# New priority offsets for the static planner of a gated linear attention and a four-expert layer

## The chip, the cores and the metric

The kernel runs on one core of one Trainium2 chip. The metric is the device time of one execution in microseconds (us); the time given is the median of three runs. The engines are named as the profile names them: PE (TensorE, with PEld for its weight loads), DVE (VectorE), ACT (ScalarE), POOL (GpSimd) and SP (SyncE, which here only issues transfers).

## The reference

Two layers stand one behind the other. The first is a gated linear attention with a 48 x 48 state for each of 4 batches and 8 heads over 768 steps; the second mixes four experts with weights that are known from the start.

```python
f = 1.0 / (1.0 + np.exp(-f_logit))
for t in range(S):                                   # S = 768
    state = f[:, :, t, :, None] * state + np.einsum('bhd,bhe->bhde', k[:, :, t], v[:, :, t])
    y[:, :, t] = np.einsum('bhd,bhde->bhe', q[:, :, t], state)
...
x = np.ascontiguousarray(y.transpose(0, 2, 1, 3)).reshape(B * S, H * D)      # 3072 x 384
p = domain_probs / (domain_probs.sum(-1, keepdims=True) + 1e-09)
for e in range(E):                                   # E = 4
    h = np.maximum(x @ w1[e], 0.0)                   # 384 -> 1024
    out += p[:, e:e + 1] * (h @ w2[e])               # 1024 -> 384
```

## The kernel before

**Tiling.** The 768 steps are cut into six chunks c = 0 to 5 of 128 steps. A chunk holds four batches b = 0 to 3, and each batch gives one tile of 128 tokens of 384 columns.

**Steps of the attention**, named `step c.b`:

- `gate1`, `gate2` (L311, L315, ACT) make the logarithm of the gate. `cs` (L319, PE) sums it over the steps into one PSUM bank. `exps` (L339, ACT, two activations for each batch, a third one, L341, in chunk 0) reads that bank and frees it.
- `q` and `k` (L347, POOL or DVE) multiply by these exponentials. `tp` turns both with a transposing transfer (L360, SP queue); in chunk 0 and half of chunk 1, `tpq`, `tpk` (L356, PE) and `ev_tp` do that.
- `at` (L383, PE) makes the scores of one batch or of a pair of batches, two PSUM banks for each batch. `ev_at0` and `ev_at1` (L387, DVE) put the mask on and free the banks.
- `y` (L394 and L398, PE) needs both `ev_at` steps of its batch. `ev_ys` (L370 on ACT, L372 on DVE) scales y by the expert weights; `xs` (L375, SP queue) turns the result into the experts' input with a transposing transfer.
- `kv` (L404, PE), `ev_kv` (L411, two instructions on DVE) and four `sf` (L416, L419, POOL) move the state on; `egs` is a small transfer for the state's factor.

**Steps of the experts.** In chunk 0 and half of chunk 1 these are `h` (L432, PE), `relu` (L443 on ACT, L441 on DVE), `o` (L447, PE), `ev_o` (L454). From the second half of chunk 1 on the work goes in groups of half a chunk and a pair of experts: `hs` (L464, PE, six matmuls of 256 columns), `relu_s` (L472 on ACT, L470 on DVE), four sums `s1` to `s4` (L482, DVE), seven products `p` (L501, PE, eight matmuls of 192 columns each), `ev_p` (L509 on DVE, L272 on ACT), and `store` (L513, SP queue). `hs c.hf.p...` reads the `xs` of both batches of half `hf`.

**What sets the order.** The function adds some 1,470 steps to a planner. A step has a cost for each engine that may run it, a priority, the steps that it depends on, and the buffers that it takes and frees. `Plan.run` goes through time: whenever an engine is free, it takes the ready step of the lowest priority. The finished list is then recorded once, so every engine gets a fixed sequence of instructions and runs it in that order on the chip, with semaphores between the engines. The planner's times decide the order and, where a step may run on several engines, the engine; on the chip nothing is chosen. PSUM is one ring of eight banks, `ps_m`; each step on PE that makes a result takes banks, and the reader of the result gives them back.

Two things tune the planner by hand. `MOVES` is a list of offsets to priorities: `cs 5.3=10.3` makes that step later, and `k 0.2=46.8@DVE` also nails the engine. And a dependency between two engines counts `LATENCY` (0.2) and the `lag` of its producer; the steps of chunk 0 on ACT and DVE carry 0.1 more:

```python
for o in self.ops:
    if o.name.split(" ")[-1].startswith("0.") and set(o.costs) & {"ACT", "DVE"}:
        o.lag += 0.1
```

**Fill-in matmuls.** Until the first `h` the recorded program puts matmuls on a constant tile (L873, 512 columns) into PE's planned pauses; their number comes from the planner's times.

## Time and profile before

| | |
|---|---|
| median of three runs | 288.67 us (288.63 to 288.93) |
| the profiled execution | 288.44 us, its span 286.7 us |
| PE busy | 280.0 us (98% of the span), 3,010 matmul records |
| DVE, ACT, POOL busy | 195.5, 180.7, 112.0 us |
| transfers | 41.85 MB |
| granted TensorE clock | 1.0 |

The profile is one execution; its span runs from the first to the last instruction, and its own time is 1.7 us longer than the span. Each digit of a row of slices is the busy share of a fortieth of the span in tenths. A group's line gives engine, line of the kernel, shapes, count, then busy time and the mean time of one instruction in ns, then the idle time of the engine before them. In the timeline, instructions of one kind that follow each other on an engine are merged into one row (start, length, count). A matmul's record runs on into its successors' by the depth of the pipeline, so what a matmul costs TensorE is read from start to start: 0.109 us for 256 columns, 0.082 us for 192.

### The profile page before, as it was taken

How to read it: one execution, taken by the hardware profiler on the slowest of the kernel's cores; microseconds unless marked ns; L12 is line 12 of the kernel's file. 1: busy time of each engine (PE TensorE's matmuls, PEld its weight loads, DVE VectorE, ACT ScalarE, POOL GpSimd, SP SyncE). 2: the span in 40 equal slices, each digit the busy share in tenths (PEclk: the TensorE clock that was granted, in tenths of full speed). 3: DMA queues.
4: the chain of work that ended last, by engine and by line, in shares of the span. 5: the costliest groups of instructions: out<-in, count | busy, mean ns of one | idle time of the engine just before them, and what ended most of it. 6: DMA issues, size and time to landing. Idle time of an engine off the chain costs nothing.

```text
span 286.7 us, 7475 instructions
## 1 busy us (share of the span) xinstructions
PE 280.0 (98%) x3010; PEld 235.7 (82%) x3016; DVE 195.5 (68%) x385; ACT 180.7 (63%) x343; POOL 112.0 (39%) x181
## 2 busy tenths in 40 slices
PE   7999999999999999999999999999999999999994
PEld 2567555567786999998999999999999999998994
DVE  4595122778698868846889876888885787630683
ACT  5847683758776846867695657375865544659500
POOL 5796500218763762478157258134373000000000
PEclk9999999999999999999999999999999999999999
DMA  7999999997998989999889999995254143420011
GB/s 154 206 173 206 207 195 201 181 198 167 176 184 161 213 154 211 128 222 195 177 182 171 126 219 179 222 184 112 58 132 90 28 84 83 88 56 2 2 55 55
DMA packets 157782, 41.85 MB, mean 146 GB/s; under 512 B 148124, under 2 KB 156956, under 8 KB 157748
## 3 DMA queue, kind: packets, MB, share of 16 engines
q1 hardware_dynamic: 146500, 34.66, 63.7%
q0 software_dynamic: 11248, 6.72, 16.5%
q8 instruction: 23, 0.38, 0.6%
q14 instruction: 11, 0.09, 0.1%
HBM read 31.51 MB, written 4.72 MB: 126 GB/s over the span
## 4 chain that ended last, share of the span: by engine, by line
PE 93%; SPq 2%; DMA 2%; DVE 1%; issue 0%; ACT 0%; DVEq 0%
PE ps_m L464 33%; PE ps_m L501 29%; PE ps_m L447 11%; PE ps_m L432 11%; SPq L282 2%; PE ps_m L383 2%; PE ps_m L398 2%; DMA q<-in_q_dram 2%; PE ps_m L394 1%; PE ps_m L404 1%; PE ps_m L319 1%; PE ps_m L356 1%; DVE AT L387 0%; ACT QK L272 0%; PE ps_m L423 0%
## 5 line engine op out<-in xcount | busy, mean ns | idle before, releaser
L464 PE MATMUL ps_m<-x,w_sb 128*128 128x256 bf16 x864 | 105.6, 273 | 0.0
L472 ACT ACTIVATE h<-ps_m 128x512 bf16<-128x512 f32 x113 | 67.2, 598 | 45.3 <-PE ps_m L464 35.9
L464 PEld LDWEIGHTS <-w_sb 128*128 128x128 bf16 x864 | 82.9, 98 | 9.1
L501 PEld LDWEIGHTS <-S 128*128 128x128 bf16 x576 | 48.6, 98 | 1.1
L509 DVE TENSOR_TENSOR o<-ps_m,o 128x192 f32<-128x192 f32 x91 | 31.2, 354 | 20.0 <-PE ps_m L501 17.7
L482 DVE TENSOR_TENSOR S<-h 128x1024 bf16<-128x1024 bf16 x36 | 28.2, 800 | 13.0 <-ACT h L472 12.9
L501 PEld LDWEIGHTS <-h 128*128 128x128 bf16 x432 | 36.3, 98 | 0.9
L447 PE MATMUL ps_m<-w_sb,h 128*128 128x384 bf16 x192 | 36.1, 326 | 0.0
L432 PE MATMUL ps_m<-x,w_sb 128*128 128x128 bf16 (+2 forms) x260 | 35.6, 281 | 0.2
L443 ACT ACTIVATE h<-ps_m 128x512 bf16<-128x512 f32 (+1 forms) x49 | 24.6, 512 | 14.0 <-PE ps_m L432 12.9
L387 DVE TENSOR_TENSOR AT<-ps_m,mask 128x512 bf16<-128x512 f32 x48 | 30.5, 683 | 4.1 <-PE ps_m L383 3.8
L419 POOL TENSOR_TENSOR Sf<-Sf,egs 48x192 f32<-48x192 f32 x40 | 20.7, 521 | 28.4 <-DVE Sf L411 23.9
L339 ACT ACTIVATE e<-ps_m 128x384 f32<-128x384 f32 x48 | 26.9, 671 | 6.3 <-PE ps_m L319 2.9
L470 DVE TENSOR_SCALAR h<-ps_m 128x512 bf16<-128x512 f32 x31 | 21.0, 691 | 12.9 <-PE ps_m L464 10.3
L432 PEld LDWEIGHTS <-w_sb 128*128 128x128 bf16 x264 | 21.8, 98 | 9.4
L347 POOL TENSOR_TENSOR qk<-q,e 128x384 bf16<-128x384 f32 x19 | 24.1, 1271 | 13.7 <-ACT e L339 6.3
L501 PE MATMUL ps_m<-ts_sb,S 128*128 128x192 bf16 x288 | 28.7, 246 | 0.0
L501 PE MATMUL ps_m<-w_sb,S 128*128 128x192 bf16 x288 | 28.5, 246 | 0.0
L501 PE MATMUL ps_m<-w_sb,h 128*128 128x192 bf16 x288 | 28.4, 246 | 0.0
L447 PEld LDWEIGHTS <-h 128*128 128x128 bf16 x192 | 18.3, 98 | 11.9 <-issue 0.4
L370 ACT ACTIVATE yb<-ps_m,pn 128x384 bf16<-128x384 f32 x49 | 26.1, 584 | 2.8 <-PE ps_m L398 2.7
L347 POOL TENSOR_TENSOR qk<-k,e 128x384 bf16<-128x384 f32 x19 | 19.4, 1023 | 14.7 <-DVE Sf L411 4.0
(74 smaller groups left out, 308.7 us busy)
## 6 DMA issues: line engine op xcount, KB each, us to landing
out_dram<-o SPq DMA_DIRECT2D x23, 192.0 KB, 2.2
w_sb<-in_moe_w_dram POOLq DMA_DIRECT2D x5, 768.0 KB, 17.3
k<-in_k_dram SPq DMA_DIRECT2D x10, 384.0 KB, 5.5
q<-in_q_dram SPq DMA_DIRECT2D x10, 384.0 KB, 5.6
v<-in_v_dram SPq DMA_DIRECT2D x10, 384.0 KB, 5.6
f<-in_f_logit_dram SPq DMA_DIRECT2D x9, 384.0 KB, 4.9
w_sb<-in_moe_w_dram POOLq DMA_DIRECT2D x6, 384.0 KB, 8.7
f<-in_f_logit_dram SPq DMA_DIRECT2D x6, 192.0 KB, 3.8
```

Source lines behind the costliest of these rows:

```text
L339: nc.scalar.activation(out=o, in_=i, func=AF.Exp, scale=1.0 if j else -1.0)
L347: return engines[eng].tensor_tensor(out=tl("qk", c, b)[:, j, :, 0:D].rearrange("t (i r) d -> t i r d", r=2), in0=tl("qk"[j], c, b // 2)[:, ...
L370: nc.scalar.activation(out=ys, in_=y, func=AF.Copy, scale=pe)
L387: nc.vector.tensor_tensor(out=tl("AT", c, b)[:, r].rearrange("s i t -> s (i t)"), in0=tl("A", c, b, r).rearrange("s i t -> s (i t)"), in1= ...
L432: nc.tensor.matmul(out=hp(c, e, fc, n0, n1, nf)[:, f], lhsT=w1_sb[:, e, kk, (fc + f) * 128:(fc + f + 1) * 128], rhs=tl("xT", c)[:, kk, n0: ...
L443: nc.scalar.activation(out=dst, in_=src, func=AF.Relu)
L447: nc.tensor.matmul(out=tl("op", c, e, nt, part)[:, cols], lhsT=tl("h", c, e, half_of(c, nt * T))[:, fc, nt * T:(nt + 1) * T], rhs=w2_sb[:, ...
L464: nc.tensor.matmul(out=out_[:, f], lhsT=w1_sb[:, e, kk, (fc + f) * 128:(fc + f + 1) * 128], rhs=tl("xs", c, hf, p)[:, el, kk, :], start=(k ...
L472: nc.scalar.activation(out=dst, in_=tl("hp", c, hf, p, el, fc), func=AF.Relu)
L482: return nc.vector.tensor_tensor(out=s(j), in0=in0, in1=in1, op=op)
L501: nc.tensor.matmul(out=out_, lhsT=lhs[:, fc, :], rhs=rhs[:, fc, :], start=(first and fc == 0), stop=(fc == KF - 1), skip_group_check=True)
L509: nc.vector.tensor_tensor(out=o, in0=src, in1=o, op=ALU.add)
```

## The change

No step, no dependency, no transfer, no buffer and no cost is added or taken away. Two things change in the planner's input. All of `MOVES` is replaced (some 200 offsets by some 200 others, many of them for the same steps), and the three lines that add 0.1 to the lag of chunk 0's steps go. The rest of the file is the same; behind those lines every line number is smaller by three.

```diff
 MOVES = (
-    "k 0.2=46.8@DVE;at 0.1=35.2;ev_xt 0.0=109.8@DVE;ev_at1 0.1=70.1;ev_y 0.3=27.8@ACT;cs 1.0=11.6;...
+    "q 0.2=5.6@DVE;at 0.1=48.9;ev_xt 0.0=34.9@DVE;ev_at1 0.1=13;ev_y 0.3=-12.9@ACT;xt 0.3=-41.9;cs 1.0=11.9;...
...
-    ...tp 2.3=-3.5;at 2.1=1.3;...hs 1.1.1.0.0=-39.6;...s1 3.1.1=10.8;s2 3.1.1=-19.8;gate1 5.2=-24.6;cs 5.2=-43.5;cs 5.3=10.3;...
+    ...exps 2.0=-33.7;exps 2.1=-19.2;...hs 1.1.0.0.6=-39.3;...s1 3.1.1=10.8;s3 3.1.1=14.7;s4 3.1.1=-1.8;cs 5.1=2.8;cs 5.3=10.5;...
...
         for o in self.ops:
             for k in o.frees:
                 self.left[k] = self.left.get(k, 0) + 1
-        for o in self.ops:
-            if o.name.split(" ")[-1].startswith("0.") and set(o.costs) & {"ACT", "DVE"}:
-                o.lag += 0.1
         left = sorted(self.ops, key=lambda o: o.prio)
```

What comes out is another recorded order on every engine. Of PE's 485 steps 319 stand in a common order; on DVE it is 189 of 352 and on ACT 174 of 314. ACT has 302 steps instead of 314, DVE 363 instead of 352, POOL 167 instead of 166; the kinds that move between ACT and DVE are `relu`, `relu_s`, `ev_ys`, `ev_p`, `ev_o`, `ev_tp` and `ev_y`. Of the SP queue's 148 transfers and placeholders 114 stand in a common order. The fill-in matmuls become 30 instead of 34.

Four stretches of the new order are named below. Written as PE issues them, before and after:

- `at 2.1`: before `at 2.1`, four `hs`, `y 2.0`, `kv 2.0`, `y 2.1`; after `at 2.1`, two `hs`, `y 2.1`, `y 2.0`.
- `hs 2.0.1.0.4`: before it follows `cs 3.1` by five steps; after `cs 3.1`, `p`, `p`, `hs 2.0.1.0.4`.
- `at 3.3`: before `at 3.3`, three `p`, `hs`, `y 3.2`; after `at 3.3`, `p`, `hs`, `y 3.2`.
- `at 4.3`: before `p`, `at 4.3`, `p`, `p`, `hs`, `p`, `hs`, `hs`, `y 4.2`, with `cs 5.2`, `cs 5.1` and `cs 5.3` all later; after `cs 5.1`, `p`, `y 4.1`, `kv 4.1`, `p`, `p`, `cs 5.2`, `p`, `cs 5.3`, `at 4.3`, `p`, `y 4.2`.

## The prediction

> **What bounds the kernel now.** I read the page first (span, busy shares, slices), then who waited for whom on TensorE, then the busy time by stretches.

> ```profile
> span 286.7 us, 7475 instructions
> PE 280.0 (98%) x3010; PEld 235.7 (82%) x3016; DVE 195.5 (68%) x385; ACT 180.7 (63%) x343; POOL 112.0 (39%) x181
> ...
> PE   7999999999999999999999999999999999999994
> ...
> PEclk9999999999999999999999999999999999999999
> ```

> ```profile
> PE ps_m L873 <- DVE S L187: 1.5, 1, 1.5
> PE ps_m L356 <- DVE qk L347: 0.6, 1, 0.6
> PE ps_m L383 <- ACT QK L272: 0.3, 1, 0.3
> PE ps_m L398 <- DVE AT L387: 0.2, 1, 0.2
> PE ps_m L873 <- issue: 0.2, 1, 0.2
> ```

> ```profile
> 88.00:96.00 8.00, 8.00 (x101) 6.45 (x100) 7.24 (x14) 6.47 (x13) 2.39 (x5) 1.00 0.97 209
> 96.00:186.00 90.00, 90.00 (x1055) 83.76 (x1053) 69.62 (x134) 59.29 (x112) 48.52 (x72) 1.00 1.00 182
> 186.00:210.00 24.00, 24.00 (x286) 22.16 (x283) 19.64 (x41) 17.67 (x34) 10.52 (x20) 1.00 0.62 118
> ```

> The second view is the whole list of TensorE's waits: 2.8 us, all of them before 20.9 us. The third has, for each stretch, its length, then PE, PEld, DVE, ACT and POOL: TensorE is busy in all of it. So after the opening there is no delay that a new order could take away, only delays that it could bring. The profiled execution took 288.44 us, 1.7 us beyond its span; the median is 288.67, 0.23 above. I add to 288.44 and then put the 0.23 back.

> **The change, part by part.** PE's work stays: the same matmuls without four fill-ins. At each place where the new order puts a step nearer to what it waits for, I compare the work left between them with the time of that chain. Rows used:

> ```profile
> 90.16 0.62 PE L383 MATMUL ps_m<-QK 48*128 48x128 bf16 x16
> 90.71 2.79 PE L464 MATMUL ps_m<-x,w_sb 128*128 128x256 bf16 x24
> ```

> ```profile
> 91.09 2.48 DVE L387 TENSOR_TENSOR AT<-ps_m,mask 128x512 bf16<-128x512 f32 x4
> ```

> ```profile
> 190.88 0.33 PE L319 MATMUL ps_m<-gp,Ub 128*128 128x384 bf16 x1
> 191.05 0.82 PE L464 MATMUL ps_m<-x,w_sb 128*128 128x256 bf16 x6
> ```

> ```profile
> 203.67 2.27 ACT L339 ACTIVATE e<-ps_m 128x384 f32<-128x384 f32 x4 [0.57 <-issue]
> ```

> ```profile
> L387 DVE TENSOR_TENSOR AT<-ps_m,mask 128x512 bf16<-128x512 f32 x48 | 30.5, 683 | 4.1 <-PE ps_m L383 3.8 <-PE ps_m L398 0.3
> L482 DVE TENSOR_TENSOR S<-h 128x1024 bf16<-128x1024 bf16 x36 | 28.2, 800 | 13.0 <-ACT h L472 12.9
> L470 DVE TENSOR_SCALAR h<-ps_m 128x512 bf16<-128x512 f32 x31 | 21.0, 691 | 12.9 <-PE ps_m L464 10.3 <-PE ps_m L501 2.3
> L372 DVE TENSOR_SCALAR yb<-ps_m,pn 128x384 bf16<-128x384 f32 x23 | 13.7, 612 | 1.1 <-PE ps_m L398 0.8 <-ACT yb L370 0.2
> L509 DVE TENSOR_TENSOR o<-ps_m,o 128x192 f32<-128x192 f32 x91 | 31.2, 354 | 20.0 <-PE ps_m L501 17.7
> ```

> From these: an `hs` or `p` costs TensorE 0.66 us (six times 0.109, eight times 0.082), a pair's `at` 0.55, `cs` 0.17 (190.88 to 191.05), `y` 0.39 and `kv` 0.16. Two `exps` back to back take ACT 2.27, one 1.18. Four mask evictions take 2.48, so they follow each other by 0.60, 0.08 less than the mean of one; I let all of DVE's instructions overlap by 0.08.

> *at 4.3 (about 198 us).* Today `cs 5.2` and `cs 5.3` come long after `at 4.3`; now `cs 5.2`, `p`, `cs 5.3` stand right ahead of it. By the ring of banks two of the four that `at 4.3` writes are those that `cs 5.2` and `cs 5.3` have just filled, and they come back only when ACT has done `exps 5.2` and `exps 5.3`. Count from the start of `cs 5.2`. TensorE would reach `at 4.3` at 0.17 + 0.66 + 0.17 + 0.1 = 1.1, but the first bank is free at 0.33 + 0.04 + 1.18 = 1.55 and the second at 0.37 + 2.27 = 2.64. So `at 4.3` stands in two halves, waits 0.45 and about 0.8, and ends near 3.0. Behind it wait one `p` and `y 4.2`, which needs DVE's two evictions of batch 2. DVE has a queue of its own there: from `relu_s 3.1.1.1.2`, released 2.7 us before `cs 5.2` (0.17 + 0.66 + 0.39 + 0.16 + 0.66 + 0.66), to `ev_at0 4.2` it must run that relu, four `ev_ys`, one `ev_kv` (two halves of about 0.35), five `ev_p` and `s1`: 0.69 + 2.45 + 0.70 + 1.77 + 0.80 less 13 overlaps = 5.3. It comes to `ev_at0 4.2` at 5.3 + 0.2 - 2.7 = 2.8 and has both done at 4.1; `y 4.2` starts at 4.2. Unhindered TensorE would be there at 1.1 + 0.55 + 0.66 = 2.3. The place costs 1.9; with an idle DVE only the bank counts (3.0 + 0.66 - 2.3 = 1.4), with DVE late by another 0.7, 2.6. I take 2.0. Today three `p` and three `hs`, 3.9 us, lie between `at 4.3` and `y 4.2`: that cover goes.

> *at 2.1 (about 91 us).* `y 2.1` needs the third eviction, `y 2.0` the fourth. In the rows above the first starts 0.93 after `at`, the third ends at 0.93 + 1.20 + 0.68 = 2.81, the fourth at 3.41. With two `hs` instead of four TensorE arrives at 0.55 + 1.31 = 1.86 and waits 1.0, then 0.2 more for the fourth. If DVE starts as soon as `at` is done (0.7), 0.2 less. The first of those `hs` also reads transposes issued behind seven of eight `ev_ys` on DVE; what it waits for those is mostly inside the same wait. I take 1.1, from 0.8 to 1.6.

> *at 3.3 and hs 2.0.1.0.4 (about 154 and 125 us).* `y 3.2` needs two evictions: 0.7 + 1.28 = 1.98 against 1.86. `hs 2.0.1.0.4` takes the bank of `cs 3.1`: 1.55 against 0.17 + 1.31 = 1.48. Each costs 0.1, from 0 to 0.3.

> *The opening (to 21 us).* The last `at` of chunk 0 now comes behind the first `h` instead of ahead of it; `q 0.1` and `k 0.1` change places between DVE and POOL (0.98 and 0.99 us in the timeline, so even); two `ev_tp` change places between ACT and DVE (1.02 and 0.69). The loads, which the chain shows until 12.8 us, and the order of the weight loads on POOL's queue are unchanged. An `h` earlier, the last `y` later: I take +0.1, from -0.8 (most of the waits of 0.6, 0.3 and 0.2 us gone) to +0.8. The fill-ins stand in pauses: four fewer cost nothing.

> *The rest.* Eleven more steps on DVE are 11 x 0.69 = 7.6 us there, 203 of 290: not the bound. In the other swaps at least two 0.66 us steps stay between producer and reader. The tail behind the last matmul is unchanged.

> Sum: 2.0 + 1.1 + 0.2 + 0.1 = 3.4, and 0.1 for a late transpose (below): 3.5. 288.44 + 3.5 = 291.9 for an execution like the profiled one; median 292.2.

> [...] In the opening the timeline has seven fill-ins in 3.17 us (1.52 to 4.67, 0.43 to 0.45 each), and five in 1.24 at 8.39 (0.22 in steady issue): half speed first, though the granted clock reads 1.0 throughout. [...]

> **Rivals.**

> *Transposes late.* On the SP queue `tp 5.0` now stands ahead of `xs 4.0.1` and `xs 4.1.0`, and waits for POOL's two products (1.27 and 1.02 us mean). `hs 4.0.0.1.6`, right behind `y 4.2`, needs `xs 4.1.0`. A transpose holds the queue 1.2 to 1.3 us and lands after 2.7 to 4.7 in this trace; with the `y` stalled its slack is near nothing. Two slow ones add 1.5 to 2.5: 293.7 to 294.7. For it: the spread of landings. Against: DMA share is only 0.62 there.

> [...]

> *Faster.* One mechanism: the opening gets dense sooner, by its full 0.8, and the stalls do not come because the readers free the banks in time. That decides only if `exps 5.2` ends within 1.1 us of `cs 5.2`'s start; ACT's 1.18 for one alone forbids it, unless the ring hands `at 4.3` other banks than I read. Then about 287.9. If the opening just balances small stalls, 288.7: the change does nothing.

> **How the numbers follow.** Forecast (three or four visible stalls, 290.3 to 293.2): 0.75. Late transposes: 0.15. Clock: 0.02. Nothing: 0.04. Faster: 0.04. Adding the low bounds, 1.4 + 0.8 + 0 - 0.8 = 1.4, gives 290.1; the high ones, 2.6 + 1.6 + 0.6 + 0.8 = 5.6, give 294.3, and late transposes reach 294.7. The range is 290.0 to 294.6. Within 0.2% (0.58 us, about what a measurement of this kernel can tell from no change): 0.04; faster 0.04; slower 0.92.

> **What would show it.** In the changed profile TensorE's list of waits gains L383 on ACT e L339 (1.0 to 1.6 us near 198), L398 on DVE AT L387 (1.2 to 1.8 us in sum, near 93, 154 and 200), perhaps L464 on DMA x. Wrong would be a list that ends with the opening, a first steady `h` more than 1 us earlier, or long stalls at places not named here.

## The result and the profile after

The changed kernel takes 293.74 us (median of four runs, 293.64 to 295.05), the kernel before beside it 288.80 (288.63 to 288.98). The ratio is 1.0175, with a 95% interval of 1.0154 to 1.0195. The profiled execution took 293.75 us, 1.75 beyond its span. The forecast was 292.2 with a range of 290.0 to 294.6: the sign and the range held, the size was 1.5 us short.

Line numbers of the changed kernel are smaller by three than those shown above: `at` is L380, `y` L391 and L395, `hs` L461, `p` L498, `cs` L316, `exps` L336, the mask eviction L384, the sums L479. First its page, the span and the granted clock in fortieths of the span:

```profile
span 292.0 us, 7464 instructions
...
PEclk9999999999999999999999999997999999999999
```

The 7 is new: in the slice from 197.1 to 204.4 us the mean clock was 0.77. TensorE's list of waits in the changed kernel (us in total, times, the longest):

```profile
PE ps_m L380 <- ACT e L336: 0.8, 2, 0.5
...
PE ps_m L461 <- ACT e L336: 0.5, 1, 0.5
PE ps_m L498 <- DVE S L479: 0.4, 1, 0.4
PE ps_m L461 <- DMA x<-yb: 0.4, 1, 0.4
```

None of these four stood in the list before, and they are all that it holds behind the opening: 2.1 us. (A wait of `y` on AT of 0.2 is in it too, at 20.6 us, as before.) The same stretches as before (length, then PE, PEld, DVE, ACT, POOL busy, granted clock, DMA share, GB/s):

```profile
88.00:96.00 8.00, 7.48 (x92) 5.70 (x91) 7.76 (x15) 4.66 (x9) 1.65 (x3) 1.00 0.93 174
...
186.00:210.00 24.00, 22.32 (x263) 19.79 (x262) 21.36 (x42) 14.38 (x26) 12.83 (x18) 0.93 0.69 129
```

TensorE now stands in two of the stretches that it filled before, and in the last one its clock is 0.93 on average. TensorE's timeline there (start, length of the record, engine, line, operation, count, idle time before it and what ended it):

```profile
196.72 0.33 PE L316 MATMUL ps_m<-gp,Ub 128*128 128x384 bf16 x1
...
198.32 0.74 PE L380 MATMUL ps_m<-QK 48*128 48x128 bf16 x9 [0.46 <-ACT e L336]
199.38 0.38 PE L380 MATMUL ps_m<-QK 48*128 48x128 bf16 x7 [0.32 <-ACT e L336]
200.18 1.32 PE L498 MATMUL ps_m<-ts_sb,S 128*128 128x192 bf16 x8 [0.42 <-DVE S L479]
...
202.50 2.09 PE L461 MATMUL ps_m<-x,w_sb 128*128 128x256 bf16 x12 [0.36 <-DMA x<-yb]
```

This is `cs 5.2`, `at 4.3` in two halves, `p 3.1.1.5`, and (behind `y 4.2`) `hs 4.0.0.1.6`, as forecast. What was not: the eight matmuls of `p` have a record of 1.32 us instead of 0.82, and inside both it and the `hs` the starts lie 0.160 and 0.214 apart instead of 0.082 and 0.109. That is half speed.

To put a number on each place I add up what the matmuls cost from start to start at full pace and take, for the same time in both traces, how far TensorE lags behind that sum, after minus before (good to about 0.2 us):

| profiled execution of | opening, to 89 us | 89 to 95 | 95 to 167 | 167 to 208 |
|---|---|---|---|---|
| the changed kernel | 0.0 | 0.9 | 0.3 | 3.9 |
| lag_back | -0.25 | 0.0 | 0.0 | 0.0 |
| kv_cost | 0.0 | 0.0 | 0.0 | 0.3 |
| latency_015 | -0.35 | 0.2 | 0.15 | 0.7 |
| cs_held | -0.6 | 0.9 | 0.3 | 1.95 |
| filled | 1.0 | 0.9 | 0.3 | 3.1 |
| tp_later | 0.4 | 0.9 | 0.3 | 2.3 |
| filled_tp | 1.7 | 0.9 | 0.3 | 3.3 |
| y_held | 0.2 | 0.5 | 0.2 | 1.5 |
| store_later | -0.3 | 0.9 | 0.3 | 2.4 |
| y_held_store | 0.2 | 0.5 | 0.05 | 1.3 |

(In filled and filled_tp the work that was put in, 2.1 us, is counted as lost. latency_015 loses 0.85 more near 226 us. The rows add up to 0.2 to 0.5 us less than the spans differ; by that the first column is some 0.2 too low throughout.) The opening spreads by 2.3 us between the lowest and the highest version. The lists of waits name `w_sb`, the weights, with 2.0 us in filled_tp and none in lag_back, so their arrival is part of it; what else is, no run settles. The times carry this spread, so for a single place I read the trace.

### The profile page after: what moved, and what is told of

Read it like the earlier page. It is cut to its first block, busy times and chain, and to the rows that moved or that the text cites. A ratio compares the mean times of both kernels' runs of the same rounds, so it can differ in the third digit from the quotient of the medians.

```text
span 292.0 us, 7464 instructions
## 1 busy us (share of the span) xinstructions
PE 281.5 (96%) x3006; PEld 236.2 (81%) x3012; DVE 200.0 (68%) x396; ACT 176.7 (61%) x331; POOL 111.6 (38%) x182
## 4 chain that ended last, share of the span: by engine, by line
PE 87%; DMA 5%; DVE 3%; SPq 2%; POOL 1%; issue 1%; DVEq 0%
PE ps_m L461 32%; PE ps_m L498 27%; PE ps_m L444 11%; PE ps_m L429 10%; DMA w_sb<-in_moe_w_dram 2%; SPq L279 2%; PE ps_m L380 2%; DMA k<-in_k_dram 1%; PE ps_m L395 1%; PE ps_m L391 1%; PE ps_m L401 1%; DMA x<-yb 1%; PE ps_m L316 1%; POOL vb L275 1%; DVE AT L384 1%; DVE yb L369 1%
## 5 line engine op out<-in xcount | busy, mean ns | idle before, releaser
L461 PE MATMUL ps_m<-x,w_sb 128*128 128x256 bf16 x864 | 107.5, 274 | 0.9 <-ACT e L336 0.5
L461 PEld LDWEIGHTS <-w_sb 128*128 128x128 bf16 x864 | 82.8, 98 | 10.6 <-PE ps_m L380 0.6
L498 PEld LDWEIGHTS <-S 128*128 128x128 bf16 x576 | 48.9, 98 | 1.8 <-DVE S L479 0.6
L498 PEld LDWEIGHTS <-h 128*128 128x128 bf16 x432 | 36.5, 98 | 0.7
L479 DVE TENSOR_TENSOR S<-h 128x1024 bf16<-128x1024 bf16 x36 | 26.5, 757 | 14.3 <-ACT h L469 14.3
L440 ACT ACTIVATE h<-ps_m 128x512 bf16<-128x512 f32 (+1 forms) x47 | 23.7, 515 | 14.4 <-PE ps_m L429 13.5
L416 POOL TENSOR_TENSOR Sf<-Sf,egs 48x192 f32<-48x192 f32 x40 | 21.7, 543 | 26.0 <-DVE S L479 13.7
L384 DVE TENSOR_TENSOR AT<-ps_m,mask 128x512 bf16<-128x512 f32 x48 | 30.6, 682 | 0.8 <-PE ps_m L380 0.6
L336 ACT ACTIVATE e<-ps_m 128x384 f32<-128x384 f32 x48 | 26.8, 668 | 7.3 <-PE ps_m L316 2.2
L498 PE MATMUL ps_m<-ts_sb,S 128*128 128x192 bf16 x288 | 29.0, 249 | 0.4 <-DVE S L479 0.4
L498 PE MATMUL ps_m<-w_sb,S 128*128 128x192 bf16 x288 | 28.0, 246 | 0.0
L498 PE MATMUL ps_m<-w_sb,h 128*128 128x192 bf16 x288 | 27.7, 246 | 0.0
L467 DVE TENSOR_SCALAR h<-ps_m 128x512 bf16<-128x512 f32 x32 | 21.7, 687 | 8.6 <-PE ps_m L461 7.2
L367 ACT ACTIVATE yb<-ps_m,pn 128x384 bf16<-128x384 f32 x43 | 22.8, 584 | 6.4 <-issue 2.9
L344 POOL TENSOR_TENSOR qk<-q,e 128x384 bf16<-128x384 f32 x18 | 22.5, 1251 | 10.6 <-ACT e L336 4.7
L344 POOL TENSOR_TENSOR qk<-k,e 128x384 bf16<-128x384 f32 x20 | 20.8, 1041 | 13.1 <-DVE qk L344 3.9
```

Source lines behind the costliest of these rows:

```text
L336: nc.scalar.activation(out=o, in_=i, func=AF.Exp, scale=1.0 if j else -1.0)
L344: return engines[eng].tensor_tensor(out=tl("qk", c, b)[:, j, :, 0:D].rearrange("t (i r) d -> t i r d", r=2), in0=tl("qk"[j], c, b // 2)[:, ...
L367: nc.scalar.activation(out=ys, in_=y, func=AF.Copy, scale=pe)
L384: nc.vector.tensor_tensor(out=tl("AT", c, b)[:, r].rearrange("s i t -> s (i t)"), in0=tl("A", c, b, r).rearrange("s i t -> s (i t)"), in1= ...
L440: nc.scalar.activation(out=dst, in_=src, func=AF.Relu)
L461: nc.tensor.matmul(out=out_[:, f], lhsT=w1_sb[:, e, kk, (fc + f) * 128:(fc + f + 1) * 128], rhs=tl("xs", c, hf, p)[:, el, kk, :], start=(k ...
```

## The experiments

The kernel before ran beside each, and there it took 289.0 to 289.6 us (medians) instead of 288.8. So ratios to it are compared. Of these 55 executions of before, ten have a mean granted clock of 0.994 and take 1.1 to 1.2 us more than the others. Over 287 us that mean is what 3.4 us at half speed amount to: this kernel, too, sometimes loses the clock. "Slower" and "won" without more refer to the changed kernel.

### Which of the two edits costs: lag_back

```diff
+        for o in self.ops:
+            if o.name.split(" ")[-1].startswith("0.") and set(o.costs) & {"ACT", "DVE"}:
+                o.lag += 0.1
         left = sorted(self.ops, key=lambda o: o.prio)
```

> The changed kernel with the three lines restored that make the planner count 0.1 us more latency behind chunk 0's steps on ACT and DVE; the new offsets stay. My theory: the offsets are fitted to that latency; without it the planner's times in chunk 0 move by a tenth, its choices flip further on, and the stalls near 91 and 198 us are such flips. Then all of them go: about 288.5 us (288.2 to 288.9), TensorE's waits end with the opening, granted clock 1.00. Rival: the new offsets are worse by themselves (they took away the steps that stood between at and y): then the waits on AT and on e stay and it takes 291 us or more.

Measured: 288.61 us (288.23 to 289.74), ratio 0.9983 (0.9970 to 0.9997). Its whole list of TensorE's waits:

```profile
PE ps_m L873 <- DVE S L187: 1.5, 1, 1.5
PE ps_m L356 <- DVE qk L347: 0.5, 1, 0.5
PE ps_m L319 <- ACT gp L315: 0.4, 1, 0.4
PE ps_m L383 <- ACT QK L272: 0.3, 1, 0.3
PE ps_m L398 <- DMA vb<-in_v_dram: 0.3, 1, 0.3
```

It ends with the opening again. So the new offsets are not at fault; as long as the planner counts that latency they are 0.17% better than the old ones, which is just clear of noise (both profiled executions have a span of 286.7 us). With it, `at 2.1` is followed by five `hs` instead of two, `cs 5.2` and `cs 5.3` come long after `at 4.3`, and `p`, `p`, `p`, `hs` lie between `at 4.3` and `y 4.2`. This is the fastest version found. The other half alone (old offsets, no latency) cannot be had: the planner reaches a state in which no step can start.

### The opening or the planner's clock: kv_cost

```diff
-            kv = P.add(f"kv {c}.{b}", {"PE": 0.22}, on(pe_kv), s15, ...
+            kv = P.add(f"kv {c}.{b}", {"PE": 0.5 if c + b == 0 else 0.22}, on(pe_kv), s15, ...
```

> The changed kernel with one number of the planner changed: kv 0.0 is reckoned at 0.50 us instead of 0.22, as much later as the restored latency makes the planner's clock there. Nothing else is issued. TensorE's order keeps the changed kernel's opening up to its 30th step and is that of the run with the latency restored behind it. My theory: what costs is not the opening but the later order, which is fitted to the planner's clock: the waits near 91 and 198 us go, 288.6 to 289.2. Rival: the other order in the opening shifts the real times of loads and weights, and the later steps wait whatever their order: 291 or more.

Measured: ratio 1.0011 (0.9993 to 1.0029); 289.75 us (288.97 to 290.98) beside 289.63 of before. The waits near 91 and 198 us are gone although TensorE's opening is the changed kernel's; from its 31st step on the order is that of lag_back. (A wait of 0.2 for x, near 168 us, is new and is the 0.3 of the table.) In the planner's own times `kv 0.0` starts at 26.17 us in the changed kernel and at 26.45 with the latency; a fictitious 0.28 us in one step, which changes nothing on the chip, gives the later order of lag_back, and that is enough. The price of the change is the later order alone.

### Is less latency the matter: latency_015

```diff
-                o.lag += 0.1
+                o.lag += 0.15
```

(against lag_back)

> The changed kernel with a latency of 0.15 us restored instead of 0.10. The planner's order on TensorE is then a third one, different from the 142nd step on from that with 0.10, and leaves two steps or fewer between at and y in three places. My theory (offsets fit one planner's clock, and any other leaves some step short of cover): slower than with 0.10 by 1.2 to 3 us, in other places than the changed kernel's, among them near 183 and 226 us. Rival (less latency makes the planner rash, more is safe): as fast as with 0.10, 288.4 to 289.2.

Measured: 291.17 us (290.10 to 293.03), ratio 1.0084 (1.0055 to 1.0114). TensorE waits 0.54 us for a `relu_s` at 183.3 us and 0.68 us for `exps` at 226.1, both where no other version waits. So more latency is not safer; the offsets fit one setting of the planner's clock. In the planner alone, without a run, TensorE's order is that of 0.10 for 0.08 to 0.12 us, and with 0.05 it is already that of the changed kernel.

### What the place at 198 us is made of: cs_held

```diff
+        at = {o.name: o for o in self.ops}
+        for a, b in (('cs 5.2', 'at 4.3'), ('cs 5.3', 'at 4.3')):
+            at[a].deps.append(at[b])
         left = sorted(self.ops, key=lambda o: o.prio)
```

> The changed kernel, with cs 5.2 and cs 5.3 held back in the planner until at 4.3 has been placed; all else the planner's. It tells what the place at 198 us costs. Bank theory alone (the two exps hold two of the four banks that at 4.3 wants): the waits on e there, 1.1 us, go and nothing takes their place: about 2 us of idling less. DVE theory alone (its queue of evictions and sums is what y 4.2 waits for): no gain. Mine, both: the waits on e go, a wait of 0.9 to 1.3 us on AT or a neighbouring DVE step takes part of their place, a gain of 0.4 to 0.8 us if the clock falls all the same (293.0 to 293.4), and of about 1.4 to 1.9 if the shorter idling leaves the clock at full speed (291.8 to 292.4).

Measured: 292.37 us (291.41 to 293.52), ratio 1.0108 (1.0084 to 1.0133), so 0.67% or 1.9 us won. In its list of waits `at` no longer waits for e, and there is

```profile
PE ps_m L501 <- DVE AT L387: 1.0, 1, 1.0
```

a `p`, at 199.14 us, whose wait is put down to a mask eviction: by the planner's list of banks it takes the one that `ev_at0 4.2` gives back. Both mechanisms are real: with the banks of `exps` taken away as a cause, DVE's queue still holds TensorE up for 1.0 us. And the clock stayed up: 1.00 in the profiled execution, 0.997 to 1.00 in all six.

### Is the half speed an answer to idling: filled

```diff
+    def fill(dst, n):
+        for _ in range(n):
+            nc.tensor.matmul(out=dst, lhsT=w1_sb[:, 0, 0, 0:128], rhs=w1_sb[:, 0, 0, 0:512], start=True, stop=True)
...
-        for i in range(NP):                                            # pe_at
+        for i in [*range(NP)] * (2 if (c, b) == (4, 2) else 1):
...
+        fill(y, 2 if (c, b) == (4, 2) else 0)                          # ahead of y 4.2
+        fill(tl("hp", c, hf, p, el, fc), 2 if (c, hf, p, el, fc) == (4, 0, 0, 1, 6) else 0)
+        fill(tl("mp", c, hf, p, bank), 2 if (c, hf, p, m) == (3, 1, 1, 5) else 0)
...
-            cs = P.add(f"cs {c}.{b}", ..., on(pe_cs), s(0),
+            cs = P.add(f"cs {c}.{b}", ..., (lambda e, b=b: [pe_cs(c, b) for _ in range(4 if (c, b) == (5, 3) else 1)]), s(0),
```

> The changed kernel with work for TensorE in the pauses near 198 us that changes no result: cs 5.3 four times instead of once, batch 2's half of at 4.3 twice, and two 128x512 products each ahead of p 3.1.1.5, y 4.2 and the hs behind it, into banks that those overwrite. No wait is removed. If the half speed from 200 to 204 us is the clock's answer to the idling, the matmuls keep their full pace there, the granted clock reads 1.00 and the kernel gains 0.8 to 1.2 us (292.5 to 293.0): what the half speed cost beyond the waits that stay. If the clock falls for another reason, nothing is gained or up to 0.5 us is lost (293.7 to 294.3).

Measured: 293.54 us (292.53 to 295.46), ratio 1.0161 (1.0130 to 1.0192): by time alone no gain is shown. The trace tells more. The eight matmuls of `p 3.1.1.5` have a record of 0.82 us again:

```profile
201.48 0.82 PE L505 MATMUL ps_m<-ts_sb,S 128*128 128x192 bf16 x8
```

The granted clock is 1.00 in the profiled execution and in all five others (0.994 in all four of the changed kernel), and from 167 to 208 us it loses 3.1 instead of 3.9 us, the gain expected (0.2 of the 3.9 lie near 168 us, where filled loses nothing). The opening of this execution happened to lose 1.0 us. So it is TensorE's idling that the clock answered to here: no wait was removed, work was put into the waits, and the clock stays up (0.997 or more in the five executions of filled_tp too).

### The transpose: tp_later and filled_tp

```diff
     done = P.run()
+    for a, side, b in (('tp 5.0', '>', 'xs 4.1.0'),):
+        o = next(o for o in done if o.name == a)
+        done.remove(o)
+        done.insert(next(i for i, x in enumerate(done) if x.name == b) + (side == '>'), o)
```

> The changed kernel with one transfer moved: the transpose tp 5.0 is issued behind xs 4.1.0 instead of two ahead of it on the SP queue, where before had it behind both too. If the late transpose costs time, the wait of hs on x near 202.5 us (0.4 us) goes and the kernel gains 0.3 to 0.5 us (293.2 to 293.4). If the hs is held by the stalls ahead of it anyway, nothing changes (293.6 to 293.8).

Measured: 293.24 us, ratio 1.0152 (1.0124 to 1.0180), and six runs in two groups: granted clock 1.00 with 292.48, 292.56 and 292.68 us, granted clock 0.994 with 293.81, 294.52 and 294.63. One kernel, with and without a loss of the clock: 1.75 us between the means. Where in the other three the clock was lost no trace shows; the place at 198 us is likely, but the kernel before has executions at 0.994 without a wait there. The median lies in the range expected only because it falls between the two groups. The profiled execution is one with a full clock:

```profile
200.35 0.83 PE L498 MATMUL ps_m<-ts_sb,S 128*128 128x192 bf16 x8 [0.41 <-DVE S L479]
...
201.87 1.47 PE L461 MATMUL ps_m<-x,w_sb 128*128 128x256 bf16 x12
```

The `hs` follows `y 4.2` without a wait, 4.97 us after the start of `cs 5.2` at 196.90. But that is not the transpose's doing: in store_later (below), where `tp 5.0` stands ahead as in the changed kernel and the clock stayed full in the profile, that distance is 5.09. By that the late transpose is worth 0.1 us, and the runs at 0.994 are no faster than the changed kernel. In the changed kernel's profile three transposes hold the queue for 5.00 us, in store_later's for 4.31: the first of them takes 2.33 us instead of 1.65, the one that the `hs` needs starts at 199.66 us, and the `hs` starts 2.84 behind it, where transposes land after 2.8 in the median. So in that execution the wait of 0.36 for x comes, by these rows, from a slow transpose.

> Both the work in the pauses near 198 us and the transpose tp 5.0 issued behind xs 4.1.0. If the clock answers to idling and the hs no longer waits for its transpose, the place costs the waits on e and on AT alone: granted clock 1.00 in every run, and 0.4 to 0.8 us less than with the filling alone (about 292.7 to 293.1), since the extra work delays exps 5.3 by some 0.3. If the filling alone had done all that can be had, no change (293.3 to 293.7).

Measured: 294.37 us (292.68 to 294.81), ratio 1.0162 (1.0137 to 1.0187), and 3.3 us from 167 to 208 beside 3.1: no gain, my expectation failed, which agrees with the transpose being worth next to nothing. (Its opening lost 1.7 us.)

### The place at 91 us: y_held, store_later, y_held_store

```diff
+        at = {o.name: o for o in self.ops}
+        for a, b in (('y 2.1', 'hs 1.1.0.0.2'), ('y 2.0', 'hs 1.1.0.0.2')):
+            at[a].deps.append(at[b])
```

> The changed kernel with y 2.1 and y 2.0 held in the planner behind the three hs that follow them in it (1.1.1.0.4, 1.1.0.0.4, 1.1.0.0.2), so that five hs stand behind at 2.1, as with the latency restored. The planner's choices behind it are its own: at 4.3 still follows cs 5.2 and cs 5.3, but with three hs between it and y 4.2 instead of one p. My theory (the stalls come from too few steps between at and y, and from banks): at 91 us 0.6 to 0.9 us are won, at 198 us the wait for S and AT goes and only waits for banks stay (0.4 to 1.0 us), the clock stays at full speed: 290.0 to 291.2. Rival: DVE is behind by itself in both places, and other steps wait in the place of y: 292.5 or more.

Measured: 291.08 us (290.72 to 294.19), ratio 1.0075 (1.0045 to 1.0104), so 1.0% or 2.9 us won by a hold near 91 us. Only 0.4 of it lies there: the waits on AT are gone, and 0.5 stay ahead of the first `hs`. The rest lies at 198 us, where the planner put three `hs` between `at 4.3` and `y 4.2` and the clock stayed up (in seven runs of eight; the one at 294.19 us has 0.993). My list of what would remain there was wrong in kind: the first `hs` behind `at 4.3` waits 0.95 us, and the profile names x, not a bank.

What are the 0.5 us? The profile names e. In the changed kernel and in kv_cost the rows are

```profile
89.06 2.26 ACT L336 ACTIVATE e<-ps_m 128x384 f32<-128x384 f32 x4 [1.67 <-issue]
...
91.44 1.47 PE L461 MATMUL ps_m<-x,w_sb 128*128 128x256 bf16 x12 [0.46 <-ACT e L336]
```

```profile
89.05 2.26 ACT L336 ACTIVATE e<-ps_m 128x384 f32<-128x384 f32 x4 [1.67 <-issue]
...
90.92 3.45 PE L461 MATMUL ps_m<-x,w_sb 128*128 128x256 bf16 x30
```

The same `hs`, in a bank that `cs 2.2` had in both, behind `exps` at the same time, starts 0.52 us earlier in kv_cost, before ACT is done at 91.3. So e is not what it waits for. What differs is the row of four transposes that it reads: SP starts it at 84.61 in the changed kernel and at 83.80 in kv_cost, and the third, the last that this `hs` needs, at 88.49 and 87.74. I took `store 0.3.0`, which is issued ahead of them, for the cause:

```diff
+    for a, side, b in (('store 0.3.0', '>', 'xs 1.3.1'),):      # as in tp_later
```

> The changed kernel with one transfer moved on the SP queue near 80 us: store 0.3.0 is issued behind the four transposes xs 1.2.0 to xs 1.3.1, as in the run with the latency restored, instead of ahead of tp 2.0 and them. The wait of the first hs behind at 2.1 (0.5 us, put down to e) is then that hs waiting for xs 1.3.0, and goes. Theory one (the y steps there are bound by DVE's evictions of at): the same 0.5 us comes back as waits on AT, no gain in time, waits on AT near 93 us of 0.7 to 0.9 us in sum. Theory two (the late transposes are the loss): 0.4 to 0.6 us are won and the waits on AT stay at 0.35.

> Both: y 2.1 and y 2.0 held behind three more hs, and store 0.3.0 issued behind the transposes. If the place at 91 us is made of these two waits and of nothing else, both are gone there (0.0 to 0.1 us of loss between 89 and 95 us, against 0.5 with the hold alone), about 0.5 us faster than the hold alone (290.5 to 290.7 beside its 291.1). If cs 2.3's bank is what the hs waits for, the 0.5 us stay.

Measured: store_later 292.94 us, ratio 1.0126 (1.0081 to 1.0170), with the wait of 0.46 unchanged; y_held_store 290.75 us, ratio 1.0058 (1.0034 to 1.0083), with 0.5 us still lost from 89 to 95. The store is innocent: without it the transposes start no more than 0.1 us earlier against the work around them. Their inputs are late, and the rows of the changed kernel and of kv_cost show which:

```profile
85.53 2.72 DVE L369 TENSOR_SCALAR yb<-ps_m,pn 128x384 bf16<-128x384 f32 x5
...
87.23 1.21 SPq L372 DMA_TRANSPOSE x<-yb  x1
```

```profile
85.08 2.19 DVE L369 TENSOR_SCALAR yb<-ps_m,pn 128x384 bf16<-128x384 f32 x4
...
85.73 1.92 SPq L372 DMA_TRANSPOSE x<-yb  x1
```

The second transpose of the row, `xs 1.2.1`, needs `ev_ys 1.2.1.1`. That is the third of the five scalings in DVE's row of the changed kernel and ends at 87.20; in kv_cost it is the first of four and ends at 85.70. In both the transpose starts 0.03 us later, and in the changed kernel the SP queue has stood since 85.83. So this scaling is 1.50 us late. Of that, 0.98 comes with `y 1.2`: TensorE issues `h 1.3.4.0` and `o 1.2.1.0` ahead of it and not behind it, so that it starts at 82.65 instead of 81.67. The other 0.52 is `ev_ys 1.3.0.1`, which now stands ahead of it on DVE. (That the row starts 0.8 later, because POOL issues `egs 2.1` ahead of `q 2.0`, is covered by this wait.) The 1.50 us shrink to 0.75 at the third transpose because the second one holds the queue for 1.92 us in kv_cost and for 1.21 in the changed kernel. This is read from the traces; no run undid the two steps alone.

### How much idling costs the clock: pauses and pauses_near

Both are the kernel of before with forced pauses of TensorE; pauses has five, pauses_near ten:

```diff
+        if o.name in pause:
+            left, flat_, ms = pause[o.name], Sf.rearrange("p b n d -> p (b n d)"), []
+            while left > 0:
+                ms.append(nc.gpsimd.memset(flat_[:, 0:min(left, 768)], 0.0))
+                left -= 768
+            after(ms[0], mms[n - 1])        # the memset waits for TensorE's last matmul
+            after(mms[n], ms[-1])           # and the step's first matmul for the memset
```

> The kernel of before with five pauses of TensorE in its last 55 us: one step of TensorE waits for a GpSimd memset that waits for the step ahead of it. The memsets have 256, 768, 1280, 1792 and 2816 columns (by the opening's rows, 0.53 us for 512, that is 0.3, 0.8, 1.3, 1.9 and 2.9 us, with some 0.2 more of hand-over), each followed by 10 us of dense work. If the clock falls when some 2 us of idling come together, the matmuls behind the fourth and fifth pause run at half pace for some microseconds and those behind the first two at full pace; if it takes 3.4 us, all run at full pace; if a short pause is enough, all but the first show it.

> The kernel of before with ten pauses of TensorE in its last 60 us, of 1.6 to 2.1 us of idling each (memsets of 1300 to 1660 columns), 4 to 9 us apart. The first such run lost its pace behind 2.2 us of idling and kept it at 1.5; a drop then lasted 3.4 us, from and to the edges of a steady grid of 3.41 us. If what counts is idling within one stretch of that grid, and the limit is about half of it (1.7 us), pauses that lie whole in one stretch with over 1.75 us of idling drop the clock from the stretch's end and those cut by an edge into two shorter pieces do not, whatever their length. If only the pause's length counted, drops would begin at one length and take all the longer ones.

Measured in pauses, 302.67 us in its one execution: behind 0.4, 0.9 and 1.5 us of idling (the waits in its timeline) the pace is full. Behind 2.08 it is half from 265.13 to 268.54 us, and behind 3.09, which end at 280.97, from 282.2 to 285.6. A third half-speed stretch, which nobody forced, lies in the opening, from 15.95 to 19.36. All three last 3.41 us, and their starts lie 73 and 5 times 3.41 us apart: in this execution the clock changed at the edges of one grid of 3.41 us. Stretches of that grid in pauses (columns as above; the clock is the third number from the right):

```profile
15.95:19.36 3.41, 3.41 (x24) 2.02 (x24) 3.41 (x7) 0.06 (x1) 3.41 (x6) 0.50 1.76 169
251.48:254.89 3.41, 2.11 (x22) 1.97 (x23) 1.44 (x3) 1.17 (x3) 1.19 (x2) 1.00 0.80 156
261.72:265.13 3.41, 1.33 (x16) 1.05 (x13) 0.18 (x1) 0.92 (x2) 1.79 (x3) 1.00 0.01 2
265.13:268.54 3.41, 3.41 (x19) 2.43 (x17) 0.00 (x0) 1.19 (x2) 0.00 (x0) 0.50 0.02 5
```

The opening is that of the kernel of before, with a wait of 1.2 us for DVE at 14.3 where the profile of before has 0.6. By the sum used for the table TensorE idles for 2.0 us in the stretch ahead, 1.35 of them in one piece (its small matmuls make this sum less sure). So the kernel of before can lose the clock there; that its executions at 0.994 did is not shown.

In pauses_near (310.52 us) one pause of ten cost the clock. Two of its grid's stretches with a whole pause in them, and the one behind the second:

```profile
244.05:247.47 3.42, 1.80 (x20) 1.48 (x17) 2.24 (x5) 1.25 (x3) 1.38 (x2) 1.00 0.45 89
278.19:281.60 3.41, 1.47 (x14) 1.08 (x13) 0.00 (x0) 1.79 (x3) 1.64 (x3) 1.00 0.00 0
281.60:285.01 3.41, 3.41 (x18) 2.42 (x17) 0.00 (x0) 1.19 (x2) 0.00 (x0) 0.50 0.00 0
```

A pause that lies whole in a stretch keeps the clock at 1.71, 1.75 and 1.78 us from start to start beyond the pace (244.05 is the last of these), and loses it at 2.10. Pauses of 2.03, 2.07 and 2.14 us that an edge cuts (the largest piece 1.44) keep it. So what counted in this execution is idling within one stretch, not the length of a pause; and the limit lay between 1.78 and 2.10 us of the 3.41, not at the 1.75 that I had expected.

The changed kernel fits. On its own grid the stretch 196.96 to 200.37 holds four pieces of idling, none over 0.65 us, 2.0 together (0.62, 0.32, 0.50 and 0.60), and the stretch behind it reads

```profile
200.37:203.78 3.41, 3.05 (x27) 2.50 (x26) 3.20 (x6) 1.05 (x2) 2.15 (x2) 0.50 0.71 137
```

By pauses_near and the changed kernel the limit lay between 1.78 and about 2.0.

In tp_later's profiled execution an edge at 200.03 cuts the same pauses, 1.7 us fall ahead of it, and the clock stays. The grid lay differently against the kernel in three executions (in the opening, half pace ends at 7.3 us in before, at 5.8 in the changed kernel, at 5.5 in tp_later), which fits that tp_later's six executions show both.

## Why the prediction was right, and where it fell short

**What bounds the kernel, and the sign.** That a new order has here "only delays that it could bring" held: both versions with a full cover between `at` and `y`, lag_back and kv_cost, are back at the time of before, within 0.2%. That 293.74 lies inside the range is partly luck: the upper bound was made of longer stalls at the places named, and what filled the gap was the clock, which the sum did not have.

**at 4.3.** The step said 2.0 (1.4 to 2.6). With a full clock the `hs` behind the place starts 4.97 and 5.09 us after `cs 5.2` in two traces; unhindered it would be 0.17 + 0.66 + 0.17 + 0.55 + 0.66 + 0.39 = 2.60. So 2.4 to 2.5: the mechanism, the two halves and both releasers as put down, the size 0.4 short. The term that was too small is DVE's queue: I had the two evictions for `y 4.2` done 4.1 us after the start of `cs 5.2`, and in the changed kernel they are done at 201.33 - 196.72 = 4.6. Its queue began 2.26 ahead of `cs 5.2`, where 2.5 was reckoned, and took 5.59 up to `ev_at0 4.2` instead of 5.3; `p 3.1.1.5` waits 0.4 for the sum ahead of them, a wait that I did not have. (The list shows 0.8 for `at` on e where 1.0 to 1.6 was named; from start to start the two waits are 0.6 and 0.5. Of the 1.2 to 1.8 us of waits of `y` on AT that were named as a sign, the list has none behind the opening: they came out ahead of `p` and of `hs`.)

**at 2.1.** 1.1 forecast, 0.9 measured, but by another split: 0.5 ahead of the first `hs`, and 0.35 on AT in pieces so short that the tails of the records (0.16 us: 0.82 for six matmuls 0.109 apart) hide them from the list of waits. Of the first part the prediction said that it is "mostly inside the same wait". That sentence failed. I counted the scalings on DVE (seven of eight by the prediction, six in the trace), but did not follow when the one that the second transpose needs is done: it comes 1.50 us late, 0.98 of it with `y 1.2`, which had moved behind two more steps, and 0.52 by the order on DVE.

**at 3.3, hs 2.0.1.0.4, the opening.** 0.10 and 0.18 us at the first two, 0.3 where 0.2 was forecast. The opening's 0.1 came out as 0.0 in the table and as 0.2 by the spans. Another 0.2 near 168 us, which I had not listed, is inside the 3.9 of the table.

**The clock.** This is the step that failed, and it carries nearly the whole error: the term was left out of the sum. A fall of the clock got 0.02. That waits of up to 1 us would leave it alone was my estimate; nothing in the trace of before showed how much idling it bears. In the changed kernel the waits counted together: 2.0 us in four pieces, none over 0.65 us, within one stretch of 3.41 us, and the clock was 0.50 in the next. (That the granted clock reads 1.0 in the opening says nothing of its first part: the trace of before has its first record of the clock at 7.3 us.) The price is one stretch at half speed, 1.7 us (half of 3.41) if TensorE is dense behind it; the means of tp_later's two groups lie 1.75 apart. In the changed kernel part of it hides in waits that were there anyway: from 196 to 208 us it loses 3.8 instead of 2.4 (tp_later's profile), so 1.4. In these 1.4 is also what the slow transpose of that execution cost, at most the 0.4 of its wait. The forecast of 292.2 and this 1.4 make 293.6.

**Transposes late.** 0.15 for it, and it is not what set the time: the place of `tp 5.0` in the queue is worth 0.1 us by the distances above, and one slow transpose in the profiled execution at most 0.4. (The landings of 2.7 to 4.7 us that the prediction reads go further in its trace: to 5.0 for `xs` and 6.0 for `tp`.)

**What the prediction did not see.** It priced the order that came out, place by place, and did not ask which of the two edits made it. The offsets alone gain 0.17%; the removed latency cost 1.9% because without it the planner's clock is 0.28 us earlier at the end of the opening.

## What to carry to other kernels

A greedy planner with hand-fitted offsets is one fit together with its costs and latencies: change one of them and offsets that were good are noise, so keep or fit them together, and look at the order behind the edit, not at the edit. Where TensorE sets the time, count for each consumer of an eviction the work that stands between producer and consumer, and follow the inputs of the step behind it as well. Count idling in sums: in the changed kernel four waits of 0.32 to 0.62 us, 2.0 us together within 3.41, cost 1.0 to 1.4 us more than their length. Harmless work put into them kept the clock up here (1.00 in all six executions of filled), though by time no gain was shown.
